# The subtraction that gives the remainder of g in the first MoE layer, issued on GpSimd in place of VectorE

## The chip, the cores and the metric

The kernel runs on one core of a Trainium2 chip. The metric is the device time of the whole program in microseconds (us), the median of several runs. Five engines work side by side, each through its own queue in the order in which the program was written: TensorE (PE in the rows; PEld is its weight load), VectorE (DVE), ScalarE (ACT), GpSimd (POOL) and SyncE (SP, which only issues transfers here). Engines wait for each other through semaphores.

## The reference: retention attention, then two MoE-like layers

Attention with a decaying state gives 3072 rows of 512 values. Two feed-forward layers follow, each of the shape 512 to 2048 to 512, with a different function g between the products. Cut to its core:

```python
for t in range(S):                                   # attention: 4 batches, 8 heads, 768 steps
    state = gamma * state + outer(k[t], v[t])
    y[t] = scale * q[t] @ state
h = x @ w_in                                         # first layer
P = a[0] + a[1]*h + a[2]*h**2 + a[3]*h**3
Q = 1 + abs(b[0])*abs(h) + abs(b[1])*h**2
x = (P / (Q + 1e-6)) @ w_out
h = x @ w_in2                                        # second layer
out = (h * clip(h + 3, 0, 6) / 6) @ w_out2
```

## The kernel before: rounded parts, remainders, and a schedule written out by hand

All matmuls run on a rounded 32-bit format. To keep the precision, each operand is held as a rounded part and a remainder: x as `xh` and `xl`, g as `gh` and `gl`, each weight tile as `hi` and `lo`. A product is then three matmuls (hi by hi, and the two mixed ones).

The rows are cut into six blocks of 512 (`blk`), and the 2048 inner columns into 16 tiles of 128 (`f`). One step handles one pair (block, f) of one layer; there are 96 steps in each layer. In step n, TensorE computes h of that step (`emit_h`, line 368, 12 matmuls), and adds the output product of the step two earlier (`emit_o`, line 392, 12 matmuls: eight that read `gh`, then four that read `gl`). In between, h goes through a chain: ScalarE makes p, s and u from h (lines 440 to 442), VectorE joins them (448, 449, 452), ScalarE makes the reciprocal r as the exponential of a negative logarithm (457, 458), VectorE finishes g in the tile p (463 to 465), ScalarE rounds it to `gh` (470), and `s_lo` makes `gl = g - gh` (line 476). The tiles p, u, gh and gl have two buffers each, so p of step n + 2 is written where p of step n lay, once `gl` of step n has been made.

The steps of the first layer run in the order: block 0 with f from 0 to 7, the whole of block 1, the rest of block 0, then blocks 2 to 5. During the first two pieces the weights of the layer are loaded and split into hi and lo, which takes ScalarE (117, 134, 138), VectorE (125, 126) and a transfer that adds while it writes (`w_lo`, line 144). That transfer is issued on GpSimd's queue, and apart from a few small memsets nothing else is on it. A loaded tile's buffer is free for the next load when that transfer has landed. Attention for the later blocks runs between the steps (lines 201 to 349): its scores `sc` and outputs `py` are short matmuls on TensorE, and ScalarE rounds the outputs to `xh` (335).

The order of each engine's queue is the order in which the loop at the end of the function calls these pieces; no scheduler moves anything. In the loop, `s_lo` of step n - 2 is called between lines 449 and 452 of step n - 1:

```python
        rest = (lambda: s_lo(k2)) if k2 and k2[0] == 0 else None
...
        if k1 and k1[0] == 0:
            s1_pq(k1, rest)
            s1_r(k1)
```

In these lines `k2[0] == 0` means the first layer; the second layer is number 1 in the code.

Of the kernel before, what the change touches and what calls it, by code (L numbers as in the profile page):

```python
# [7 lines left out]
F32 = mybir.dt.float32  # L8
# [4 lines left out]
ALU = mybir.AluOpType  # L13
# [18 lines left out]
def tile_retention_moe_moe2(  # L32
# [13 lines left out]
    nc = tc.nc  # L46
# [310 lines left out]
    hps, tm, gsp, acc = {}, {}, {}, {}  # L357
# [115 lines left out]
    def s_lo(key):  # L473
        gh = gsp[key]
        gl = g_p.tile([128, NB], F32R, tag="gl", name="gl" + "_".join(map(str, key)))
        nc.vector.tensor_tensor(out=gl, in0=tm.pop(key), in1=gh.bitcast(F32), op=ALU.subtract)  # L476
        gsp[key] = (gh, gl)


# [226 lines left out]
    for n in range(len(steps) + LAG):  # L706
# [19 lines left out]
        if k2 and k2[0] == 0:  # L726
            s1_g(k2)
            s_hi(k2)
        elif k2:
            s_lo(k2)  # L730
# [6 lines left out]
        while made["lo"] < made["bits"]:  # L737
            w_second()
        rest = (lambda: s_lo(k2)) if k2 and k2[0] == 0 else None
        if k1 and k1[0] == 1:  # L740
            if rest:
# [99 lines left out]
```

## Time and profile before

| what | value |
|---|---|
| time, median of 3 runs (lowest, highest) | 1170.91 us (1170.37, 1173.07) |
| span of the profiled execution, first to last instruction | 1169.4 us |
| TensorE busy | 1142.6 us, 98% of the span |
| VectorE busy | 754.3 us, 64% |
| ScalarE busy | 640.2 us, 55% |
| GpSimd busy | 32.6 us, 3% |

The profiled execution has no time of its own beside its span; the median of the timed runs lies 1.5 us above that span. Shares are means over the whole program, which has three stretches with different limits: attention of block 0 up to about 40 us, the first layer up to about 645 us (with the weights of the layer being prepared up to about 150 us), and the second layer.

### The profile page before, as it was taken

How to read it: one execution, taken by the hardware profiler on the slowest of the kernel's cores; microseconds unless marked ns; L12 is line 12 of the kernel's file. 1: busy time of each engine (PE TensorE's matmuls, PEld its weight loads, DVE VectorE, ACT ScalarE, POOL GpSimd, SP SyncE). 2: the span in 40 equal slices, each digit the busy share in tenths (PEclk: the TensorE clock that was granted, in tenths of full speed). 3: DMA queues.
4: the chain of work that ended last, by engine and by line, in shares of the span. 5: the costliest groups of instructions: out<-in, count | busy, mean ns of one | idle time of the engine just before them, and what ended most of it. 6: DMA issues, size and time to landing. Idle time of an engine off the chain costs nothing.

```text
span 1169.4 us, 15740 instructions
## 1 busy us (share of the span) xinstructions
PE 1142.6 (98%) x6028; PEld 931.0 (80%) x6028; DVE 754.3 (64%) x1174; ACT 640.2 (55%) x1091; POOL 32.6 (3%) x43
## 2 busy tenths in 40 slices
PE   8698999999999999999999999999999999999998
PEld 5566788888888888888888788888888888888886
DVE  6898898998888878888899865432332332332322
ACT  3898888866666566666888644332222332332222
POOL 0121110000000000000000000000000000000000
PEclk9898999999999999999999999999999999999999
DMA  9898643312112113121332643120200200200000
GB/s 334 246 263 211 183 114 95 135 53 74 46 46 82 46 55 117 46 81 37 108 99 64 227 136 106 36 90 1 72 1 1 72 1 1 72 1 1 36 1 36
DMA packets 59547, 100.20 MB, mean 86 GB/s; under 512 B 5328, under 2 KB 23888, under 8 KB 59472
## 3 DMA queue, kind: packets, MB, share of 16 engines
q1 hardware_dynamic: 54144, 89.50, 23.2%
q0 software_dynamic: 5328, 9.70, 4.8%
q8 instruction: 47, 0.77, 0.3%
q14 instruction: 28, 0.23, 0.1%
HBM read 73.76 MB, written 15.73 MB: 77 GB/s over the span
## 4 chain that ended last, share of the span: by engine, by line
PE 80%; ACT 8%; DVE 7%; DMA 2%; issue 2%; SPq 0%; ACTq 0%; DVEq 0%
PE h L368 38%; PE accA L392 19%; PE accB L392 19%; DMA T<-in_qk_t_dram 2%; PE sc L236 1%; PE py L272 1%; DVE u L463 1%; ACT r L457 1%; DVE p L464 1%; DVE p L448 1%; ACT r L458 1%; DVE u L449 1%; PE py L300 1%; ACT p L440 1%; ACT u L442 1%
## 5 line engine op out<-in xcount | busy, mean ns | idle before, releaser
L368 PE MATMUL h<-xh,wi 128*128 128x512 f32 x1536 | 416.4, 393 | 0.9 <-ACT xh L335 0.9
L368 PEld LDWEIGHTS h<-xh,wi 128*128 128x128 f32 x1536 | 285.8, 188 | 63.9 <-issue 2.7
L368 PE MATMUL h<-xl,wi 128*128 128x512 f32 x768 | 205.7, 390 | 0.0
L488 DVE SCALAR_TENSOR_TENSOR g<-r,h 128x512 f32<-128x512 f32 x96 | 66.1, 688 | 169.4 <-ACT r L482 168.7
L368 PEld LDWEIGHTS h<-xl,wi 128*128 128x128 f32 x768 | 144.3, 188 | 30.7
L482 ACT ACTIVATE r<-h,cst 128x512 f32<-128x512 f32 x96 | 66.0, 687 | 183.6 <-PE h L368 183.1
L470 ACT ACTIVATE gh<-g 128x512 fp32r<-128x512 f32 x96 | 60.7, 632 | 153.1 <-PE accB L392 113.9
L476 DVE TENSOR_TENSOR gl<-g,gh 128x512 fp32r<-128x512 f32 x96 | 66.5, 693 | 120.3 <-ACT gh L470 120.3
L392 PE MATMUL accA<-gh,wo 128*128 128x512 f32 x384 | 120.5, 395 | 8.3 <-ACT gh L470 8.3
L392 PE MATMUL accB<-gh,wo 128*128 128x512 f32 x384 | 119.4, 392 | 0.0
L392 PE MATMUL accB<-wo,gh 128*128 128x512 f32 x384 | 118.3, 390 | 0.0
L392 PE MATMUL accA<-wo,gh 128*128 128x512 f32 x384 | 118.2, 389 | 0.0
L440 ACT ACTIVATE p<-h,ab 128x512 f32<-128x512 f32 x96 | 74.3, 774 | 38.5 <-PE h L368 35.3
L392 PEld LDWEIGHTS accA<-gh,wo 128*128 128x128 f32 x384 | 71.7, 189 | 26.7 <-ACT gh L470 12.5
L457 ACT ACTIVATE r<-u,cst 128x512 f32<-128x512 f32 x96 | 69.2, 721 | 38.2 <-DVE u L449 38.2
L476 DVE TENSOR_TENSOR gl<-p,gh 128x512 fp32r<-128x512 f32 x96 | 65.8, 685 | 33.3 <-ACT gh L470 33.1
L392 PEld LDWEIGHTS accB<-gh,wo 128*128 128x128 f32 x384 | 72.7, 189 | 15.4
L392 PEld LDWEIGHTS accB<-wo,gh 128*128 128x128 f32 x384 | 72.1, 188 | 15.0
L392 PEld LDWEIGHTS accA<-wo,gh 128*128 128x128 f32 x384 | 72.1, 188 | 14.9
L470 ACT ACTIVATE gh<-p 128x512 fp32r<-128x512 f32 x96 | 60.7, 632 | 35.1 <-DVE p L465 35.0
L448 DVE TENSOR_TENSOR p<-p,h 128x512 f32<-128x512 f32 x96 | 65.5, 682 | 16.3 <-ACT u L442 16.1
L392 PE MATMUL accA<-wo,gl 128*128 128x512 f32 x192 | 74.8, 389 | 0.0
(76 smaller groups left out, 1441.5 us busy)
## 6 DMA issues: line engine op xcount, KB each, us to landing
rwi<-in_moe_w_in_dram SPq DMA_DIRECT2D x32, 512.0 KB, 4.5
rwo<-in_moe_w_out_dram SPq DMA_DIRECT2D x32, 512.0 KB, 3.9
T<-in_qk_t_dram SPq DMA_DIRECT2D x48, 256.0 KB, 4.0
kv<-in_kv_dram SPq DMA_DIRECT2D x32, 256.0 KB, 4.8
x<-o SPq DMA_DIRECT2D x24, 256.0 KB, 2.4
xr<-x SPq DMA_DIRECT2D x24, 256.0 KB, 4.2
out_dram<-o SPq DMA_DIRECT2D x20, 256.0 KB, 2.0
wi<-rwi POOLq DMA_DIRECT2D x19, 256.0 KB, 3.8
```

Source lines behind the costliest of these rows:

```text
L236: nc.tensor.matmul(banks[e][:, p * CH : (p + 1) * CH], lhsT=kT[rows, p, :], rhs=qT[rows, p, :], start=True, stop=True)
L272: nc.tensor.matmul(to(e, j, i), lhsT=vr[:, 2 * p + e, :], rhs=am[:, e * NP + p, :], start=j == 0, stop=first and j == 1, skip_group_check= ...
L300: nc.tensor.matmul(to(e, j, i), lhsT=state[rows, p * D : (p + 1) * D], rhs=qT[rows, p, :], start=False, stop=j == 1, skip_group_check=True,)
L368: nc.tensor.matmul(ps, lhsT=w[:, cs], rhs=x[:, c, :], start=n == 0, stop=n == 3 * KD - 1)
L392: nc.tensor.matmul(acc[layer, blk][j], lhsT=l, rhs=r, start=f == f0 and i == 0, stop=f == f1 and i == 2)
L440: nc.scalar.activation(p, h, AF.Identity, scale=ab[:, 3:4], bias=ab[:, 2:3])
L448: nc.vector.tensor_tensor(out=p, in0=p, in1=h, op=ALU.mult)
L457: nc.scalar.activation(r, u, AF.Ln, scale=1.0 / LN_SCALE, bias=ln_bias)
L470: nc.scalar.activation(gh, tm[key], AF.Copy)
L476: nc.vector.tensor_tensor(out=gl, in0=tm.pop(key), in1=gh.bitcast(F32), op=ALU.subtract)
L482: nc.scalar.activation(r, hps[key], AF.Relu, bias=three)
L488: nc.vector.scalar_tensor_tensor(out=g, in0=r, scalar=6.0, in1=h, op0=ALU.min, op1=ALU.mult)
```

## The change: one instruction of each step of the first layer goes to another engine

The subtraction in `s_lo` is issued on GpSimd when the layer is the first one, and stays on VectorE in the second. Its operands, its tiles and the place of the call in the program are as before. It concerns 96 instructions of 128 partitions by 512 elements.

```diff
@@ -473,7 +473,8 @@
     def s_lo(key):
         gh = gsp[key]
         gl = g_p.tile([128, NB], F32R, tag="gl", name="gl" + "_".join(map(str, key)))
-        nc.vector.tensor_tensor(out=gl, in0=tm.pop(key), in1=gh.bitcast(F32), op=ALU.subtract)
+        engine = nc.gpsimd if key[0] == 0 else nc.vector
+        engine.tensor_tensor(out=gl, in0=tm.pop(key), in1=gh.bitcast(F32), op=ALU.subtract)
         gsp[key] = (gh, gl)
```

GpSimd's queue in the first steps, before the change. The names are those of the tiles (kind and layer, then f, then a running number): the weights' remainders, each row one transfer that adds.

```order
L144 DMA wi0_2_414<-rwi0_2_166 128x512
L144 DMA wo0_1_431<-rwo0_1_168 128x512
L144 DMA wi0_3_480<-rwi0_3_175 128x512
L144 DMA wo0_2_500<-rwo0_2_434 128x512
L144 DMA wi0_4_545<-rwi0_4_436 128x512
L144 DMA wo0_3_570<-rwo0_3_438 128x512
L144 DMA wi0_5_637<-rwi0_5_440 128x512
```

The same place after the change (the lines of the file below the edit are one higher):

```order
L144 DMA wi0_2_414<-rwi0_2_166 128x512
L144 DMA wo0_1_431<-rwo0_1_168 128x512
L144 DMA wi0_3_480<-rwi0_3_175 128x512
L144 DMA wo0_2_500<-rwo0_2_434 128x512
L477 ISA
L477 TENSOR_TENSOR gl0_0_0_550<-p0_0_469,gh0_0_0_539 128x512
L144 DMA wi0_4_545<-rwi0_4_436 128x512
L144 DMA wo0_3_570<-rwo0_3_438 128x512
L477 TENSOR_TENSOR gl0_0_1_642<-p0_1_532,gh0_0_1_630 128x512
L144 DMA wi0_5_637<-rwi0_5_440 128x512
```

The first subtraction stands behind the transfer of wo 2 and ahead of that of wi 4. Ahead of it stands an instruction without operands, ISA, which the builder put there by itself; it stands there once, ahead of the first subtraction only.

ScalarE's queue at line 440 of the third step, which writes p of f = 2 into the buffer of p of f = 0; the names in brackets are the engines whose semaphores an instruction waits for (- before, + after):

```order
 L134 ACTIVATE wo0_3_570<-rwo0_3_438 128x512 [waits DVE_49]
 L138 ACTIVATE wo0_3_570<-wo0_3_570 128x512 [waits Activation_49]
-L440 ACTIVATE p0_2_623<-h0_0_2_517,ab_96 128x512 [waits PE_49]
+L440 ACTIVATE p0_2_623<-h0_0_2_517,ab_96 128x512 [waits PE_49,Pool_49]
 L441 ACTIVATE s0_2_621<-h0_0_2_517 128x512
 L442 ACTIVATE u0_2_622<-h0_0_2_517,ab_96 128x512
```

Nothing moves there, but the instruction now also waits for GpSimd, and so does line 440 of the later steps of the layer.

VectorE's queue in the second step, where the call stands between lines 449 and 452:

```order
 L448 TENSOR_TENSOR p0_1_532<-p0_1_532,h0_0_1_397 128x512
 L449 SCALAR_TENSOR_TENSOR u0_1_531<-s0_1_530,babs_97,u0_1_531 128x512
-L476 TENSOR_TENSOR gl0_0_0_550<-p0_0_469,gh0_0_0_539 128x512
 L452 SCALAR_TENSOR_TENSOR p0_1_532<-p0_1_532,ab_96,h0_0_1_397 128x512
 L247 TENSOR_TENSOR T1_1_1_127<-sc1_1_508,tab_95 128x1024
```

The subtraction is gone and the rows behind it move up by one.

## Rows read from the trace of the kernel before

**Rows 1.** The page's first part: busy time, share and instructions of each engine.
```profile
PE 1142.6 (98%) x6028; PEld 931.0 (80%) x6028; DVE 754.3 (64%) x1174; ACT 640.2 (55%) x1091; POOL 32.6 (3%) x43
```

**Rows 2.** Windows: stretch, length, busy PE, PEld, DVE, ACT, POOL (instructions), clock, DMA share, GB/s.
```profile
40.00:110.00 70.00, 59.76 (x364) 46.31 (x365) 65.44 (x106) 66.90 (x130) 14.02 (x16) 0.90 0.93 242
...
200.00:300.00 100.00, 100.00 (x524) 81.78 (x524) 91.10 (x141) 69.83 (x116) 0.00 (x0) 1.00 0.24 83
300.00:400.00 100.00, 100.00 (x621) 81.25 (x620) 84.59 (x131) 63.35 (x104) 0.00 (x0) 1.00 0.20 64
...
40.00:45.00 5.00, 1.98 (x16) 1.81 (x16) 4.89 (x9) 4.82 (x9) 0.90 (x1) 0.50 0.97 273
45.00:50.00 5.00, 5.00 (x21) 4.09 (x20) 4.44 (x8) 4.97 (x10) 0.90 (x1) 0.83 1.08 311
```

**Rows 3.** The chain that ended last, 28 to 135 us: start, length, what ran.
```profile
54.91 0.29 ACT p L440
...
57.15 0.49 ACT xh L335
...
128.10 0.53 ACT gh L470
```

**Rows 4.** Groups by line: operation, tiles, count | busy us, mean ns | idle before.
```profile
L476 DVE TENSOR_TENSOR gl<-p,gh 128x512 fp32r<-128x512 f32 x96 | 65.8, 685 | 33.3 <-ACT gh L470 33.1
...
L622 ACT ACT_TABLE_LOAD x1 | 1.3, 1283 | 0.7 <-PEq L818 0.7
```

**Rows 5.** Timeline of GpSimd, 44 to 64 us: start, length, instruction, idle before.
```profile
45.70 0.90 POOL L144 DMA_DIRECT2D wo<-rwo  x1 [2.33 <-ACT wo L138]
50.26 0.86 POOL L144 DMA_DIRECT2D wi<-rwi  x1 [3.66 <-ACT wi L138]
```

**Rows 6.** Timeline of TensorE's matmuls, 48 to 58 us.
```profile
49.99 0.61 PE L392 MATMUL accB<-gh,wo 128*128 128x512 f32 x2
50.44 0.62 PE L392 MATMUL accA<-gl,wo 128*128 128x512 f32 x2
...
52.56 0.67 PE L300 MATMUL py<-T,state 64*64 64x128 f32 x16
```

**Rows 7.** Timeline of ScalarE, 46 to 60 us.
```profile
47.60 0.62 ACT L470 ACTIVATE gh<-p 128x512 fp32r<-128x512 f32 x1
...
54.81 0.77 ACT L440 ACTIVATE p<-h,ab 128x512 f32<-128x512 f32 x1
...
57.03 0.61 ACT L335 ACTIVATE xh<-py 128x512 fp32r<-128x512 f32 x1
```

**Rows 8.** Transfers issued from 30 to 110 us: queue, count, KB each, us to landing.
```profile
rwi<-in_moe_w_in_dram SPq DMA_DIRECT2D x10, 512.0 KB, 5.1
...
wo<-rwo POOLq DMA_DIRECT2D x9, 256.0 KB, 6.0
...
kv<-in_kv_dram SPq DMA_DIRECT2D x2, 256.0 KB, 7.0
```

**Rows 9.** Timeline of TensorE's matmuls, 92 to 112 us.
```profile
98.65 1.22 PE L392 MATMUL accA<-gh,wo 128*128 128x512 f32 x2 [3.52 <-ACT gh L470]
...
102.23 1.05 PE L392 MATMUL accA<-gl,wo 128*128 128x512 f32 x2
103.08 1.05 PE L392 MATMUL accB<-gl,wo 128*128 128x512 f32 x2
```

**Rows 10.** Timeline of ScalarE, 76 to 112 us: where VectorE ended its idle time.
```profile
85.64 0.63 ACT L134 ACTIVATE wi<-rwi 128x512 fp32r<-128x512 f32 x1 [0.76 <-DVE rwi L126]
...
103.76 0.63 ACT L470 ACTIVATE gh<-p 128x512 fp32r<-128x512 f32 x1 [0.42 <-DVE p L465]
```

**Rows 11.** Windows of line 476 alone: stretch, length, VectorE busy (count), clock, DMA share, GB/s.
```profile
40.00:110.00 70.00, 5.47 (x8) 0.90 0.93 242
...
200.00:300.00 100.00, 11.66 (x17) 1.00 0.24 83
300.00:400.00 100.00, 10.98 (x16) 1.00 0.20 64
```

**Rows 12.** Timeline of all engines in one step of the first layer, 336 to 341 us.
```profile
336.97 0.69 DVE L476 TENSOR_TENSOR gl<-p,gh 128x512 fp32r<-128x512 f32 x1 [2.76 <-ACT gh L470]
...
338.75 0.78 ACT L440 ACTIVATE p<-h,ab 128x512 f32<-128x512 f32 x1 [0.54 <-PE h L368]
...
340.37 0.62 PE L392 MATMUL accA<-gl,wo 128*128 128x512 f32 x2
```

## The prediction

> **What bounds the kernel now.** I read the page's totals first: TensorE is busy 98% of the span and GpSimd 3% [rows 1], so time can only be won where TensorE waits. The windows say where that is. From 200 us on TensorE is busy all the time, 100.00 of 100, although VectorE still has 91.10 and 84.59 of 100 [rows 2]. VectorE is lighter after the change, but there nobody waits for it, and I cost the relief at nothing. From 40 to 110 us it is otherwise: TensorE 59.76 of 70, VectorE 65.44, ScalarE 66.90, and the transfer engines 0.93 busy [rows 2]. The chain that ended last shows which of them decides: it stands on ScalarE at 54.91 and 57.15 and goes over to TensorE through gh at 128.10 [rows 3]. So a delay of ScalarE between about 50 and 128 us reaches the end of the program in full, and VectorE gives time back only where ScalarE waits for it.
>
> **What is removed.** 96 subtractions of 685 ns leave VectorE, 65.8 us in all [rows 4]. In the stretch where this can count, ScalarE's idle time that VectorE ended is 0.76 us at 85.64 and 0.42 us at 103.76 [rows 10]. Elsewhere up to 110 us ScalarE has its own queue to work through. The gain is thus at most about 1.2 us, and I take 1.2; its lower end is 0, if the blocking below eats it.
>
> **What the same subtraction costs on GpSimd.** The trace has no computing instruction of this size there. Below, it is bounded by VectorE's own 0.69 us; above, by three passes at that pace (two inputs and an output one after the other), 2.06 us. I take the middle, 1.4 us. In the long stretch there is room for it: in the step at 336.97 the subtraction starts at 336.97, p's buffer is wanted by line 440 at 338.75 and TensorE reads gl at 340.37 [rows 12], 1.78 and 3.40 us later. Even 2.06 us would delay line 440 by only 0.3 us. I cost the other 95 subtractions at nothing; their cover is TensorE's matmuls on gh, and without that cover each would cost its excess over 0.69 us, 0.7 us.
>
> **The first one is different.** Ahead of it stands, once, an instruction that no other row in the neighbourhood has, ISA. I read it as GpSimd fetching the program for its first computing instruction. No row shows its price. The nearest row below is ScalarE's table load, 1.28 us [rows 4]. Above, I allow a software transfer in flight to be waited out and then the slowest landing of this stretch: 6.0 + 7.0 = 13 us [rows 8]. Whatever has to come from memory here comes through transfer engines that are 0.93 busy [rows 2], where a weight tile needs 5.1 us to land [rows 8]. I take two such landings in a row, one to look up and one to fetch, 10.2 us. That is my choice between the ends, nearer to the landings than to the table load.
>
> The Trainium skill (GPSIMD Engine Reference, section 2.1 Instruction dispatch) says that the first call of a freshly loaded routine pays some 6 us for loading its code, and that the profile shows no instruction for it. By that figure the first subtraction would end at about 54 us and the sum would be near 1171 us, an estimate; no run here has shown it so far.
>
> Now the times. GpSimd comes to the ISA when the transfer of wo 2 is issued, at 45.70 + 0.90 = 46.60 [rows 5]. It is not kept busy before gh of the first step is there, at 47.60 + 0.62 = 48.22 [rows 7], but the fetch then lasts to 46.60 + 10.2 = 56.8, and the first gl is ready at 56.8 + 1.4 = 58.2. Before, TensorE read it at 50.44 [rows 6].
>
> Who is late next: TensorE ends its matmuls on gh at 49.99 + 0.61 = 50.6 [rows 6] and then stands for 7.6 us. ScalarE wants p's first buffer again at 54.81 [rows 7] and now waits for GpSimd, 3.4 us. Behind that it wants the attention output py for xh at 57.03 [rows 7], and py stands behind the late gl matmuls on TensorE. From the first gl matmul at 50.44 to the end of py at 52.56 + 0.67 = 53.23 is 2.8 us at full clock [rows 6]. After an idle time of 3.52 us before 98.65 TensorE's pairs of matmuls took 1.05 us [rows 9], not 0.62 [rows 6]: the granted clock had fallen from 2.4 to 1.2 GHz, and it had also fallen at 40 to 45 us (0.50, then 0.83 in the next 5 us) [rows 2]. At the lower level all the way the same work takes 5.6 us. I take 4.2 us, half of it slow. So py is done at 58.2 + 4.2 = 62.4, and ScalarE takes it 62.4 - 57.03 = 5.4 us late. The 3.4 us of p are inside this, not added to it.
>
> The transfers on GpSimd's queue behind the first subtraction are late too: that of wi 4 was issued at 50.26 [rows 5] and now comes at 58.2, 7.9 us late, and with it the loads that wait for its buffer. ScalarE itself is 5.4 us late by then, so 2.5 us more must be hidden by the loads being ahead of their use; I cost that at nothing, and if this lead is too short it adds up to 2.5 us.
>
> **The sum.** Against the profiled execution: 1169.4 + 5.4 - 1.2 = 1173.6 us of span; the median of the runs lies 1.5 us above this span, which gives 1175.1, and I say 1175 us, 0.35% slower. With the low end of the load (1.28 us) gl is ready by 49.6 and nothing is late: 1170.9 - 1.2 = 1169.7. With the high ends (13, 2.06 and 5.6 us) py is 46.60 + 13 + 2.06 + 5.6 - 57.03 = 10.2 us late, and with no gain the time is 1181.1.
>
> **Rivals.** A change of less than 0.2%, 2.3 us here, is about what a measurement of this kernel cannot tell from none.
>
> 1. A short load. If the ISA takes one landing of 5.1 to 7.0 us [rows 8], gl is ready at 53.1 to 55.0, TensorE stands for 2.5 to 4.4 us, and py is 0 to 2.2 us late (with 2.8 us of matmuls, and with 4.2). Less the 1.2 us of relief this gives 1169.7 to 1171.9: the same. For it speaks that one landing is all that a single fetch would need; against it, that the engines which would carry it are 0.93 busy with other work [rows 2].
>
> 2. Faster. The ISA costs nothing, because it prepares nothing or GpSimd has the program already. Then VectorE's relief stands alone: 1169.7 us. If ScalarE's chain also comes early enough that TensorE's idle time before 98.65 is too short for the clock to fall, the 6 pairs at 0.85 us from start to start (102.23 to 103.08) [rows 9] go back to the 0.45 us of 49.99 to 50.44 [rows 6], which is 2.4 us more: 1167.3. It decides from the point where the load ends before about 49 us, when gl is as early as on VectorE. Against it: ScalarE works almost all of the stretch, 66.90 of 70 [rows 2], so the relief does not reach it.
>
> 3. Blocking. If GpSimd and VectorE can't both read at once, each subtraction stops VectorE for its whole 1.4 us. In 200 to 300 us VectorE would have 91.10 - 11.66 + 17 x 1.4 = 103.2 of 100 [rows 2, 11], and in 40 to 110 us 65.44 - 5.47 + 8 x 1.4 = 71.2 of 70, together 4.4 us more; in 300 to 400 us 84.59 - 10.98 + 16 x 1.4 = 96.0 still fits. It begins to hurt there at 1.65 us. On top of the forecast: 1179.5 us. Against it: the subtraction starts when gh is there, and next to that VectorE mostly stands at lines 448 and 452, which read h, or waits.
>
> The Trainium skill (SBUF — State Buffer, section Who interferes with whom) has this as a rule: a VectorE instruction with two SBUF inputs and a GpSimd instruction that reads SBUF lock each other out, and the later one waits for the whole of the first. By that rule lines 449 and 463 to 465 are concerned and lines 448 and 452, which read h in PSUM, are not; no run here shows it yet.
>
> **How the numbers follow.** The long load has 0.50, with 1175 us and its own range of 1173 to 1178; a tenth of it falls within 0.2%. The short load has 0.24, nearly all of it within 0.2%. Faster, or no load, has 0.12: half of it by more than 0.2%, half within. Blocking on top, or a load above 13 us, has 0.14, all but a hundredth slower. Together: faster 0.08, same 0.34, slower 0.58. The range reaches from 1169.5, which leaves out the better half of rival 2, to 1180, which leaves out the upper part of the blocking and the highest loads.
>
> **What would show it.** In the changed kernel's timeline GpSimd's first subtraction ends between 56 and 60 us, long after its gh; TensorE stands before its gl matmuls from about 50.6 us; line 440 of the third step waits for GpSimd; the granted clock falls behind it; xh follows some 5 us late; and from 200 us on each step is as long as before, with the subtraction at about 1.4 us and VectorE's rows unchanged in length. I am wrong if the first gl comes before 53 us, if ScalarE's lateness at 57 us is made up by 128 us, or if TensorE waits for gl again and again behind 150 us.

## The result and the profile after

The changed kernel takes 1179.42 us (median of four runs, 1177.38 to 1179.83) against 1170.64 us (1169.99 to 1173.07) for the kernel before in the same session. The ratio is 1.007, with a 95% interval of 1.0056 to 1.0085: 0.75% slower, where the forecast was 0.35%. The direction was right, but by luck: it had been forecast from a loss that did not arise, as the rows below show.

The page's first part of the changed kernel, to be read beside [rows 1]:

```profile
PE 1145.3 (97%) x6028; PEld 930.8 (79%) x6028; DVE 734.3 (62%) x1078; ACT 640.4 (54%) x1091; POOL 171.9 (15%) x139
```

VectorE has 96 instructions fewer, but its busy time fell only from 754.3 to 734.3 us. The 96 subtractions were worth 65.8 us [rows 4]. Added up one by one, VectorE's other instructions grew by 35 us; the remaining 11 us or so are short overlaps of neighbouring records, which busy time counts once and of which there are fewer now. The page's groups say where the largest part of the growth went (operation, tiles, count | busy us, mean ns | idle before). First two groups of the kernel before:

```profile
L449 DVE SCALAR_TENSOR_TENSOR u<-s,babs,u 128x512 f32<-128x512 f32 x96 | 71.5, 745 | 0.0
...
L457 ACT ACTIVATE r<-u,cst 128x512 f32<-128x512 f32 x96 | 69.2, 721 | 38.2 <-DVE u L449 38.2
```

The changed kernel:

```profile
L477 POOL TENSOR_TENSOR gl<-p,gh 128x512 fp32r<-128x512 f32 x96 | 138.5, 1442 | 395.6 <-ACT gh L470 237.7
...
L457 ACT ACTIVATE r<-u,cst 128x512 f32<-128x512 f32 x96 | 69.4, 723 | 61.8 <-DVE u L449 61.7
L449 DVE SCALAR_TENSOR_TENSOR u<-s,babs,u 128x512 f32<-128x512 f32 x96 | 101.4, 1056 | 0.0
```

Line 449 (u = |b| s + u, both inputs in SBUF) is untouched by the diff, and its mean went from 0.745 to 1.056 us, 30 us over 96 of them. Lines 448 and 452, which read h in PSUM, stayed within 0.002 us of their means before. ScalarE's wait for line 449, ahead of line 457, grew from 38.2 to 61.7 us.

First the place where the forecast put its loss. This is the changed kernel's timeline from 45 to 60 us (start, length, instruction, idle before), to be read beside [rows 5 to 7]:

```profile
48.82 0.64 ACT L470 ACTIVATE gh<-p 128x512 fp32r<-128x512 f32 x1
...
49.55 1.29 POOL L477 TENSOR_TENSOR gl<-p,gh 128x512 fp32r<-128x512 f32 x1 [1.72 <-ACT gh L470]
...
52.58 0.62 PE L392 MATMUL accA<-gl,wo 128*128 128x512 f32 x2
...
58.62 0.61 ACT L335 ACTIVATE xh<-py 128x512 fp32r<-128x512 f32 x1
```

The first subtraction begins 0.09 us behind gh (48.82 + 0.64 = 49.46) and takes 1.29 us like the others. gl is ready at 50.84 and TensorE reads it at 52.58 without standing. What the queue does ahead of it has rows of its own; this is line 477 by operation (count: min/median/max ns, first to last start in us):

```profile
L477 POOL TENSOR_TENSOR gl<-p,gh x96: 1267/1422/1753, 49.5 to 653.0; 128x512 fp32r<-128x512 f32 x96
...
L477 POOLq MODIFY_POOL_CONFIG  x2: 398/398/398, 47.5 to 47.5; - x2
```

Two settings of 0.398 us at 47.5 us, while GpSimd waits for gh anyway, stand where I had put a fetch of 10.2 us.

Where the time is lost instead shows in three windows cut at the same steps in both kernels. They hold 24, 58 and 14 of the 96 executions of line 449; weights are prepared in the first and in the last, hardly any in the middle. Each window ends where TensorE starts the same group of matmuls of line 368. First the kernel before (stretch, length, busy PE, PEld, DVE, ACT, POOL, clock, DMA share, GB/s):

```profile
40.00:207.60 167.60, 155.94 (x953) 123.69 (x954) 151.33 (x242) 149.61 (x285) 23.48 (x27) 0.96 0.68 179
207.60:565.30 357.70, 357.41 (x2098) 291.23 (x2097) 307.13 (x473) 234.97 (x382) 0.86 (x1) 1.00 0.21 70
565.30:648.10 82.80, 82.55 (x361) 67.21 (x360) 79.47 (x127) 69.30 (x117) 6.03 (x7) 1.00 0.37 94
```

The changed kernel:

```profile
40.00:213.50 173.50, 157.17 (x953) 124.05 (x954) 153.05 (x220) 151.95 (x287) 55.73 (x51) 0.96 0.67 173
213.50:571.00 357.50, 357.30 (x2098) 291.00 (x2096) 289.98 (x413) 232.31 (x380) 85.17 (x59) 1.00 0.21 70
571.00:656.80 85.80, 84.41 (x361) 66.99 (x362) 75.67 (x114) 71.36 (x120) 29.42 (x23) 1.00 0.35 92
```

The first stretch is 5.9 us longer (1.2 us of it are there at 25 us already, ahead of any changed instruction), the middle is 0.2 us shorter, the last 3.0 us longer: 8.7 us, against spans of 1169.4 and 1178.0. Line 449 alone in the same windows (stretch, length, VectorE busy), before:

```profile
40.00:207.60 167.60, 17.89 (x24) 0.96 0.68 179
207.60:565.30 357.70, 43.21 (x58) 1.00 0.21 70
565.30:648.10 82.80, 10.43 (x14) 1.00 0.37 94
```

and changed:

```profile
40.00:213.50 173.50, 31.20 (x24) 0.96 0.67 173
213.50:571.00 357.50, 56.63 (x58) 1.00 0.21 70
571.00:656.80 85.80, 13.58 (x14) 1.00 0.35 92
```

It grew by 13.3, 13.4 and 3.2 us. In the middle, where TensorE is busy 357.30 of 357.50 us, the same growth costs nothing. TensorE's busy share alone doesn't mark the last stretch, though: it was busy there 82.55 of 82.80 us before. What sets this stretch apart in the kernel before is that TensorE's weight loads wait there for `gh` four times, 1.4 us in all, and in the whole middle once, 0.2 us.

Single instructions show how it grows. Eight rows of the changed kernel's timeline, from 186 to 196 us and from 347 to 361 us:

```profile
188.88 1.28 POOL L477 TENSOR_TENSOR gl<-p,gh 128x512 fp32r<-128x512 f32 x1 [3.97 <-issue]
...
189.33 1.39 DVE L126 SCALAR_TENSOR_TENSOR rwo<-rwo 128x512 int32<-128x512 int32 x1 [0.92 <-ACT rwo L117]
...
190.75 0.63 ACT L134 ACTIVATE wo<-rwo 128x512 fp32r<-128x512 f32 x1 [1.46 <-DVE rwo L126]
...
193.83 1.09 PE L272 MATMUL py<-T,kv 128*64 128x128 f32 x16 [0.96 <-DVE T L247]
...
347.19 1.28 POOL L477 TENSOR_TENSOR gl<-p,gh 128x512 fp32r<-128x512 f32 x1 [2.94 <-issue]
347.25 1.78 DVE L449 SCALAR_TENSOR_TENSOR u<-s,babs,u 128x512 f32<-128x512 f32 x1
...
353.39 0.75 DVE L449 SCALAR_TENSOR_TENSOR u<-s,babs,u 128x512 f32<-128x512 f32 x1
353.68 1.62 POOL L477 TENSOR_TENSOR gl<-p,gh 128x512 fp32r<-128x512 f32 x1 [5.20 <-ACT gh L470]
```

At 347.19 GpSimd starts first and keeps its 1.28 us; line 449 starts 0.06 us later and takes 1.78 us, and ends 0.56 us behind the subtraction. At 353.39 line 449 starts first and keeps its 0.75 us; the subtraction takes 1.62 us. At 188.88 it is line 126 that is second (1.39 us where it has 0.69 alone); ScalarE waits 1.46 us for it, and VectorE comes late to T, for which TensorE waits 0.96 us at 193.83. The meetings of six lines in the changed kernel, counted from the timeline between the first and the last subtraction (median us of the VectorE instruction; "GpSimd first" means that GpSimd's instruction started first):

```
line                    no meeting   GpSimd first   VectorE first (GpSimd then)
449 (s and u in SBUF)   18x 0.745    36x 1.777      41x 0.746 (1.615)
126 (raw weights)       18x 0.693     3x 1.389      12x 0.694 (1.423)
508 (xr and xh)          4x 0.680     3x 1.127       1x 0.691 (1.295)
215 (T and tq)          16x 0.678     2x 1.126      -
448 (h in PSUM)         59x 0.681    12x 0.681      23x 0.687 (1.288)
452 (h in PSUM)         53x 0.735    41x 0.742       1x 0.742 (1.306)
```

The Trainium skill has this rule (SBUF — State Buffer, section Who interferes with whom): a VectorE instruction with two inputs in SBUF and a GpSimd instruction that reads SBUF exclude each other, whoever is first. The trace agrees with it for lines 449, 126, 508 and 215 against 448 and 452. I had this rule as rival 3. Two more lines met the subtraction in a way that the table leaves out. Line 463 has two inputs in SBUF too and started 13 times in the last 0.13 us of a subtraction; it took 0.693 us as always and ended 0.57 us behind the subtraction, no earlier than a held line 449 does. Line 125, which reads a single tile in SBUF, started once under a subtraction and took 1.251 us instead of 0.421, so two inputs are not the only case that is held.

### The profile page after: what moved, and what is told of

It is laid out like the page before. It is cut to its first block, busy times and chain, and to the rows that moved or that the text cites. A ratio compares the mean times of both kernels' runs of the same rounds, so it can differ in the third digit from the quotient of the medians.

```text
span 1178.0 us, 15879 instructions
## 1 busy us (share of the span) xinstructions
PE 1145.3 (97%) x6028; PEld 930.8 (79%) x6028; DVE 734.3 (62%) x1078; ACT 640.4 (54%) x1091; POOL 171.9 (15%) x139
## 4 chain that ended last, share of the span: by engine, by line
PE 75%; DVE 11%; ACT 8%; issue 4%; DMA 1%; SPq 0%; POOLq 0%; ACTq 0%; DVEq 0%
PE h L368 35%; PE accA L392 18%; PE accB L392 18%; DVE u L449 2%; DVE p L448 2%; ACT r L457 2%; DVE u L463 2%; DVE p L464 2%; PE py L272 1%; ACT r L458 1%; PE sc L236 1%; DVE p L465 1%; ACT kv L224 1%; PE py L300 1%; DVE T L247 1%
## 5 line engine op out<-in xcount | busy, mean ns | idle before, releaser
L477 POOL TENSOR_TENSOR gl<-p,gh 128x512 fp32r<-128x512 f32 x96 | 138.5, 1442 | 395.6 <-ACT gh L470 237.7
L457 ACT ACTIVATE r<-u,cst 128x512 f32<-128x512 f32 x96 | 69.4, 723 | 61.8 <-DVE u L449 61.7
L449 DVE SCALAR_TENSOR_TENSOR u<-s,babs,u 128x512 f32<-128x512 f32 x96 | 101.4, 1056 | 0.0
L463 DVE SCALAR_TENSOR_TENSOR u<-u,r 128x512 f32<-128x512 f32 x96 | 66.0, 687 | 46.3 <-ACT r L458 46.3
```

The costliest lines, as they stand in the source:

```text
L449: nc.vector.scalar_tensor_tensor(out=u, in0=s, scalar=babs[:, 1:2], in1=u, op0=ALU.mult, op1=ALU.add)
L457: nc.scalar.activation(r, u, AF.Ln, scale=1.0 / LN_SCALE, bias=ln_bias)
L463: nc.vector.scalar_tensor_tensor(out=u, in0=u, scalar=Q_CONST, in1=r, op0=ALU.add, op1=ALU.mult)
L477: engine.tensor_tensor(out=gl, in0=tm.pop(key), in1=gh.bitcast(F32), op=ALU.subtract)
```

## Experiments

The theory now: the loss comes from VectorE instructions with two SBUF inputs being held by GpSimd's subtraction, above all line 449, and only in stretches where ScalarE's chain sets TensorE's pace. Its rivals: a preparation ahead of GpSimd's first subtraction (my forecast), and the later gl by itself, 1.28 us instead of 0.69.

**An early first call.** One subtraction of one column on GpSimd at the program's start, so that anything that a first call must prepare is over by 47 us.

```diff
+    first = const.tile([128, 1], F32, name="first")
+    nc.gpsimd.tensor_tensor(out=first, in0=three, in1=three, op=ALU.subtract)
```

> The changed kernel with one more subtraction on GpSimd, of one column, right behind the memsets at the start, so that whatever the first computing instruction needs is done before the stretch from 25 us on. Theory of the late first subtraction (the prediction's): the load leaves the path and the time falls by most of the 8.8 us, to about 1172 us. Theory of blocking (a VectorE instruction with two SBUF inputs and the subtraction on GpSimd exclude each other): no change, 1179 us within 1.5 us, and line 449 still at a mean of about 1.06 us.

Measured: 1178.46 us (1177.85 to 1180.15), ratio to before 1.0068 [1.0053, 1.0083]. Nothing comes back. The timeline of GpSimd in this kernel at the first subtraction of line 477:

```profile
48.17 1.29 POOL L477 TENSOR_TENSOR gl<-p,gh 128x512 fp32r<-128x512 f32 x1 [1.70 <-ACT gh L470]
```

It waits 1.70 us for gh and takes 1.29 us; without the early call it was 1.72 and 1.29. The early call itself, GpSimd's first subtraction in this kernel, starts at 0.95 us, 0.10 us behind its two settings, and takes 0.19 us. The load theory falls.

**Line 449 with one input in SBUF.** The changed kernel with line 449 reading h in PSUM instead of u, and the same edit in the kernel before. The term |b0| h is thereby left out of the denominator, so the computation differs from the reference in that term; instructions, sizes and order are the same.

```diff
-        nc.vector.scalar_tensor_tensor(out=u, in0=s, scalar=babs[:, 1:2], in1=u, op0=ALU.mult, op1=ALU.add)
+        nc.vector.scalar_tensor_tensor(out=u, in0=s, scalar=babs[:, 1:2], in1=h, op0=ALU.mult, op1=ALU.max)
```

> The changed kernel, but line 449 takes h from PSUM as its second input in place of u from SBUF, with a maximum in place of the addition, so the term with the absolute value of b0 is left out of Q. Theory of blocking: line 449 is no longer held and is back at about 0.745 us, subtractions that start under it fall from 1.6 to 1.3 us, and only line 126 and a few others are still held; of the 8.8 us between 1 and 4 are left, 1172 to 1175 us. Theory of latency (gl is ready 0.7 us later in each step, whatever VectorE does): the loss stays at 7 to 9 us over the same edit without GpSimd.

> The kernel before with the same edit of line 449 (h from PSUM and a maximum; the term with the absolute value of b0 is left out), the base for the run beside it. Both theories: 1170.6 us within 2 us, since line 449 costs the same 0.74 us with either input, as line 452 does with h.

Measured: the changed kernel with the edit takes 1170.95 us, ratio 1.0001 [0.9992, 1.0011]; the kernel before with it 1171.47 us, ratio 1.0001 [0.9992, 1.0010]. The whole loss is gone, where I had expected 1 to 4 us to be left, and the edit by itself is worth nothing. Lines 449 and 477 by operation in the changed kernel with the edit:

```profile
L449 DVE SCALAR_TENSOR_TENSOR u<-s,babs,h x96: 734/741/744, 40.8 to 640.7; 128x512 f32<-128x512 f32 x96
...
L477 POOL TENSOR_TENSOR gl<-p,gh x96: 1268/1292/1434, 48.5 to 646.0; 128x512 fp32r<-128x512 f32 x96
```

None of the 96 is above 0.744 us, though 61 of them began under a running subtraction. Its three windows:

```profile
40.00:209.70 169.70, 154.80 (x953) 122.63 (x954) 139.80 (x220) 149.63 (x285) 54.09 (x50) 0.97 0.68 177
209.70:567.10 357.40, 357.24 (x2097) 291.00 (x2095) 277.42 (x413) 231.25 (x380) 75.07 (x59) 1.00 0.21 70
567.10:649.80 82.70, 82.14 (x361) 67.55 (x362) 72.50 (x114) 70.99 (x120) 27.00 (x23) 1.00 0.36 96
```

The last stretch is back at 82.7. The first is 2.1 us longer in this one execution, while the timed medians are equal: that is about how far single executions differ in this stretch. GpSimd's subtraction still takes 1.29 us here, 0.6 us more than VectorE's, so the rival of the later gl falls too. What is gone as well are the subtractions of some 1.6 us that line 449 held (their mean is 1.304 us here and 1.442 in the changed kernel); but in the changed kernel TensorE stood for gl only once in the whole program, 0.7 us. Lines 126 and 508 were still held in this kernel (three times each, 1.386 and 0.991 us), and lines 125 and 215 once each, so it is line 449 that carries the loss.

**Which steps lose.** GpSimd takes the subtractions of the middle steps only (54 of 96; the first pair of lines), or those of the other 42 only (the second pair).

```diff
-        engine = nc.gpsimd if key[0] == 0 else nc.vector
+        engine = nc.gpsimd if 26 <= at_of[key] < 80 else nc.vector
...
-        engine = nc.gpsimd if key[0] == 0 else nc.vector
+        engine = nc.vector if key[0] == 1 or 26 <= at_of[key] < 80 else nc.gpsimd
```

> The subtraction on GpSimd only in steps 26 to 79 of the first layer, where no weights are prepared and TensorE is busy all the time, and on VectorE in the other 42. Theory of blocking: VectorE is held there as much as in the changed kernel (line 449 at about 1 us on average) but has room for it, so 1170.6 us within 1.5 us. Theory of latency: 54 of 96 subtractions come later, so about half of the loss, 1175 us. Theory of the late first subtraction: the first one falls into a stretch with slack, so 1170.6 us too.

> The complement of the middle steps: the subtraction on GpSimd only in steps 0 to 25 and 80 to 95 of the first layer, where weights are prepared, on VectorE in the 54 between. Theory of blocking where there is no room: the whole loss, 1178 to 1180 us. Theory that the loss comes evenly with the number of subtractions: 42 of 96 of it, 1174.5 us.

Measured: the middle alone 1171.61 us, ratio 1.0002 [0.9992, 1.0011]; the two ends alone 1178.63 us, ratio 1.0064 [1.0049, 1.0079]. The middle alone is not free of holds; line 449 in that kernel:

```profile
L449 DVE SCALAR_TENSOR_TENSOR u<-s,babs,u x96: 742/746/1780, 41.1 to 640.0; 128x512 f32<-128x512 f32 x96
```

13 of them are at some 1.78 us, and cost nothing. The three windows of the kernel with the ends alone:

```profile
40.00:212.10 172.10, 155.21 (x952) 122.55 (x953) 153.03 (x220) 151.43 (x286) 55.31 (x51) 0.97 0.67 175
212.10:569.50 357.40, 357.27 (x2097) 291.00 (x2095) 305.32 (x467) 234.54 (x380) 6.06 (x5) 1.00 0.21 70
569.50:655.30 85.80, 84.40 (x360) 66.96 (x361) 75.59 (x114) 71.49 (x120) 29.42 (x23) 1.00 0.34 93
```

Beside the kernel before they are 4.5 us longer, 0.3 us shorter and 3.0 us longer, the pattern of the full change.

**The subtraction behind line 449.** The changed kernel with a one-column copy of u on GpSimd ahead of each subtraction, so that it begins when line 449 of the next step is through.

```diff
+        if behind is not None:
+            nc.gpsimd.tensor_copy(out=gate, in_=tm[behind][1][:, 0:1])
...
+        rest = (lambda: s_lo(k2, k1 if k1[0] == 0 else None)) if k2 and k2[0] == 0 else None
```

> The changed kernel, with a copy of one column of u on GpSimd ahead of each subtraction, so that the subtraction can't start before line 449 has ended; it then runs beside lines 452, 247 and 342, which take one input from SBUF. Theory of blocking by line 449: line 449 is back at 0.745 us in every step, the subtraction at 1.3 us, and most of the loss is gone, 1171 to 1174 us; what is left would be gl coming later than TensorE wants it where there is little room. Theory that the subtraction's length on GpSimd is the cost: as in the changed kernel or worse, 1179 us or more.

Measured: 1174.88 us (1173.78 to 1177.66), ratio 1.0035 [1.0025, 1.0046]: somewhat more than half of the loss comes back, and I had expected most of it (1171 to 1174 us). Line 449 and line 215 in this kernel, by operation:

```profile
L449 DVE SCALAR_TENSOR_TENSOR u<-s,babs,u x96: 735/745/749, 40.7 to 641.0; 128x512 f32<-128x512 f32 x96
...
L215 DVE TENSOR_TENSOR T<-T,tq x16: 1187/1537/1546, 90.2 to 519.4; 128x512 f32<-128x512 f32 x16
```

Line 449 is never held, but the hold has moved: all 16 of this group of line 215 now meet the subtraction (0.68 us alone). These holds don't carry the rest of the loss. The three windows of this kernel, cut at the same steps:

```profile
40.00:207.40 167.40, 156.54 (x953) 122.64 (x953) 141.37 (x220) 150.42 (x285) 55.85 (x73) 0.97 0.68 180
207.40:566.30 358.90, 357.62 (x2098) 291.10 (x2097) 287.42 (x415) 235.77 (x383) 84.74 (x117) 1.00 0.21 70
566.30:651.00 84.70, 83.40 (x362) 67.04 (x361) 75.35 (x113) 70.69 (x117) 26.95 (x36) 1.00 0.35 94
```

Beside the kernel before they are 0.2 us shorter, 1.2 and 1.9 us longer. When line 215 is through (519.4 us) nothing is lost: up to 559.27 us TensorE starts the same group of line 368 within 0.01 us of the kernel before. What is lost behind that goes with a gl that comes too late for TensorE, once for 1.28 us at 565.24 and four times in the last stretch. TensorE's and VectorE's waits from 566.3 to 651 us (us in all, times, longest):

```profile
PE accA L392 <- POOL gl L479: 1.2, 4, 0.7
PEld accA L392 <- POOL gl L479: 3.6, 6, 1.1
...
DVE u L463 <- POOL gl L479: 6.5, 7, 0.9
```

Line 463, which overwrites u, starts only when the subtraction behind the copy has ended: in the step at 602.42 us the copy ends at 602.46, the subtraction at 603.71, and line 463 starts at 603.74. TensorE's standing for gl, 2.5 us in these five waits, is near to the 2.8 us by which this execution is longer; what line 463's waits have in it was not taken apart.

**No line 449.** The changed kernel and the kernel before with line 449 taken out: ScalarE forms u as one square of a scaled and shifted |h|, and the constants go into lines 457 and 463.

```diff
-        nc.scalar.activation(s, h, AF.Square)
-        nc.scalar.activation(u, h, AF.Abs, scale=ab[:, 4:5])
+        nc.scalar.activation(s, h, AF.Abs)
+        nc.scalar.activation(u, s, AF.Square, scale=root[:, 0:1], bias=root[:, 1:2])
...
-        nc.vector.scalar_tensor_tensor(out=u, in0=s, scalar=babs[:, 1:2], in1=u, op0=ALU.mult, op1=ALU.add)
...
```

> The changed kernel without line 449: ScalarE makes the whole of u as one square of a scaled and shifted absolute value of h (the constant that is too much goes into the constants of lines 457 and 463), so VectorE has 96 instructions of 0.745 us less and none with two SBUF inputs beside the subtraction. Theory of blocking: the loss is gone, and in the stretch where weights are prepared some of the time that ScalarE spent waiting for line 449 is won as well, 1168 to 1171 us. Theory of latency: 7 to 9 us over the run beside it that has the subtraction on VectorE.

> The kernel before without line 449, made in the same way, the subtraction on VectorE. VectorE has 66 us less to do; where TensorE is busy all the time that is worth nothing, and where weights are prepared ScalarE decides, so 1168.5 to 1171 us: at most the 2 us or so that ScalarE waited for VectorE there. If VectorE had been the bound there, 1160 us or less.

Measured: with GpSimd 1176.45 us (1174.93 to 1177.90), ratio 1.0045 [1.0029, 1.0061]; without it 1172.85 us (1171.85 to 1177.00), ratio 1.0019 [1.0009, 1.0030]. Both missed what I expected. Taking 96 instructions off VectorE made the kernel before 0.2% slower. In its profiled execution ScalarE is 2.3 us late ahead of the first step already (line 440 started at 38.13 us, the same instruction, now line 441, at 40.44), behind the eight small instructions that the edit adds at 28.4 us. The square of s also takes ScalarE 0.816 us where line 442 took 0.69. What either is worth was not tested. With GpSimd there is still a loss, 1176.45 - 1172.85 = 3.6 us, less than half of the change's 8.8. Line 216 in the kernel with GpSimd (215 before):

```profile
L216 DVE TENSOR_TENSOR T<-T,tq x16: 684/1745/1754, 92.9 to 523.5; 128x512 f32<-128x512 f32 x16
```

As with the copy, the hold has moved on to the next line with two SBUF inputs. That it carries these 3.6 us is not shown: ten of its held executions lie between 260 and 530 us, and cut at the same steps the two kernels differ by 2.6 us in the first stretch (172.1 against 169.5), 0.5 in the middle and 0.8 in the last. What carries them stays open.

**Another piece of work for GpSimd.** The kernel before with the sign change of the weights on GpSimd instead of ScalarE, to look for a faster kernel than both.

```diff
-        nc.scalar.activation(lo, hi.bitcast(F32), AF.Copy, scale=-1.0)
+        nc.gpsimd.tensor_scalar(out=lo, in0=hi.bitcast(F32), scalar1=-1.0, scalar2=None, op0=ALU.mult)
```

> The kernel before with the 37 sign changes of the weights' rounded parts (the line that writes lo = -hi, 0.633 us each on ScalarE) computed on GpSimd, and the rest of g left on VectorE. This looks for a version faster than both. ScalarE is the busiest engine in the first stretch (82.09 of 88 us from 40 to 128 us), and 37 x 0.633 = 23.4 us would leave it, about half of them ahead of the stretch in which TensorE bounds. If the limit there is ScalarE's sum: 1 to 3 us faster, 1168 to 1170 us. If holding decides: a sign change reads one tile in SBUF on GpSimd, so it holds every VectorE instruction with two inputs in SBUF that begins under it, lines 449, 126 and 215 again, for up to 1 us each; with 37 of them instead of 96, some 15 to 20 holds, a third of the change's loss, against the gain: 1170 to 1174 us, and the mean of line 449 between 0.75 and 0.90 us.

Measured: 1174.17 us (1173.51 to 1176.06), ratio 1.0027 [1.0017, 1.0037]. ScalarE's busy time in the stretch from 40 to 128 us fell from 82.09 to 69.91 us, and the kernel is slower: 12 us off ScalarE did not pay for what came with them. Lines 138 and 449 in this kernel:

```profile
L138 POOL TENSOR_SCALAR wi<-wi x19: 1479/1783/2046, 34.4 to 643.2; 128x512 fp32r<-128x512 f32 x19
L138 POOL TENSOR_SCALAR wo<-wo x18: 1479/1820/1955, 37.7 to 632.4; 128x512 fp32r<-128x512 f32 x18
...
L449 DVE SCALAR_TENSOR_TENSOR u<-s,babs,u x96: 739/744/754, 40.0 to 642.9; 128x512 f32<-128x512 f32 x96
```

My mark for holding, a mean of line 449 above 0.75 us, did not come: here line 449 always started first and GpSimd was the one held. VectorE's gl, which has two SBUF inputs, was second 19 times and took 1.098 us instead of 0.683. Which counts for the 3.4 us, these holds or the sign change being 1.1 us longer ahead of the weight's last transfer, stays open. No version faster than the kernel before was found.

## Why the prediction was right in direction and wrong in cause

- **What bounds the kernel** held in part. The stretch from 207 to 565 us lost nothing, with 58 subtractions on GpSimd and 13.4 us of holds in it. But "From 200 us on TensorE is busy all the time" was read from 200 to 400 us, and the last stretch, from 565 us, lost 3.0 us although TensorE is busy there 82.55 of 82.80 us: it follows ScalarE's chain through gh all the same.
- **The relief of 1.2 us** can't be seen: with the holds taken away the ratio is 1.0001 [0.9992, 1.0011]. It is below what the timing tells, or nothing. The sum had also left out a third wait of ScalarE for VectorE in its stretch, 0.99 us ahead of line 440 at 108.47.
- **1.4 us for the subtraction** was close: 1.28 us alone, 1.442 us on average with its own holds.
- **The step that failed is the fetch**: "I take two such landings in a row, one to look up and one to fetch, 10.2 us." The trace of the changed kernel has two settings of 0.398 us in its place, in idle time; the first gl was ready at 50.84 us and not at 58.2, before the 53 us that I had named as the sign of being wrong, and TensorE did not stand. xh came at 58.62 us instead of 57.03, 1.6 us later and not 5.4, and 1.2 us of this were there before. The early call shows the same: nothing to save. I had read a price into an instruction whose rows gave none, and chosen a value near the slow end. The Trainium skill's figure for a first call (GPSIMD Engine Reference, section 2.1 Instruction dispatch, some 6 us) does not show here either: the first subtraction starts 0.09 us behind its input and takes 1.29 us.
- **"I cost the other 95 subtractions at nothing"** was wrong too, and it is here that the 8.8 us arise. I had asked whether gl would be late for its readers, and it hardly was (0.7 us, once); I had not asked what VectorE does while GpSimd reads.
- **Rival 3 was the mechanism**, at 0.14 with the high loads. My sentence against it failed: that VectorE stands mostly at lines 448 and 452 beside the subtraction. Line 449 lies between these two, and 77 of 96 times it met the subtraction. Its price failed as well. I had added whole subtractions to VectorE's sum per window and looked for an overflow from 200 to 300 and from 40 to 110 us. The sum never overflowed, VectorE's busy time even fell; what counted was that line 449 is a link in the chain s, u, r, gh, so where that chain decides each hold moves ScalarE and then TensorE. That its 1179.5 us come so near to the measured 1179.42 is luck: they add 4.4 us of overflow to the late xh of the fetch, and neither came.

The waits show that chain in the last stretch. First the kernel before, 565.3 to 648.1 us:

```profile
ACT r L457 <- DVE u L449: 4.8, 7, 0.7
...
PEld accA L392 <- ACT gh L470: 1.4, 4, 0.7
```

The changed kernel, the same view, 571 to 656.8 us:

```profile
ACT r L457 <- DVE u L449: 7.5, 14, 0.7
...
PEld accA L392 <- ACT gh L470: 3.9, 8, 0.9
PEld accA L392 <- POOL gl L477: 1.1, 1, 1.1
```

ScalarE now waits for line 449 in all 14 steps, and TensorE's weight loads stand 2.5 us longer for gh, most of the 3.0 us that this stretch lost. Of the first stretch's 5.9 us, 1.2 were there before the change could act; from 40 to 213 us TensorE's weight loads wait 1.2 us more for gh (11.0 to 12.2) and 2.5 us more for T of line 247 (2.1 to 4.6).

## What to carry to other kernels

Before work goes to GpSimd beside VectorE, list the VectorE instructions with two inputs in SBUF that can run at the same time, and ask of each whether a longer duration is on the chain: a hold can cost most of a GpSimd instruction there (1.03 us beside a subtraction of 1.28), whatever VectorE's total says. Don't go by TensorE's busy share alone in asking that: two stretches in which it was busy over 99% behaved differently. With one input of line 449 in PSUM its holds were gone, and the loss with them. Shifting the GpSimd work in time moved the holds to another line, where they cost nothing, but made its result late for TensorE, which did. An instruction without a visible price in the trace should be bounded by a run that contains it, not by the slowest thing nearby.

## What the runs showed of the hardware

The hold works both ways, and the first to start is untouched: line 449 took 1.777 us instead of 0.745 behind a running subtraction, and the subtraction 1.615 us instead of 1.288 behind a running line 449. It is nearly whole: a held line 449 ended some 0.55 us behind the subtraction's end, where it takes 0.745 us alone. With one of its inputs in PSUM, line 449 met the subtraction 77 times with no effect on either (0.741 and 1.290 us). Line 125, an int32 shift that reads one tile in SBUF, was held in its one meeting with the subtraction (1.251 us instead of 0.421). On GpSimd a sign change of one 128x512 tile, with one input, took longer (1.479 us at least) than the subtraction of two (1.267 us at least).
